# A scan and a routed expert layer on one core: x laid out in zero-padded blocks, one product per two heads, routing pieces placed last in a tile

## The chip, the core and the metric

The kernel runs on one core of a Trainium2 chip. The core has five engines that run side by side and meet through semaphores: TensorE (matrix products, with a queue of its own for weight loads), VectorE, ScalarE, GpSimd and SyncE, which here only issues DMA transfers. [...] Times are microseconds of device time for one execution. In the views, PE is TensorE, PEld its weight loads, DVE is VectorE, ACT is ScalarE, POOL is GpSimd and SP is SyncE; a letter q behind a name is that engine's sequencer. L556 is line 556 of the kernel before.

## What is computed

Two layers follow one another. The first is a chunked state-space scan over 4 batches, 8 heads, 768 positions, with 32 values and 16 states per head. The second sends each of the 3072 tokens, with the 8 x 32 = 256 values that the scan gives for it, to one of 8 experts by a hash of its token id, and applies that expert's two matrices with a ReLU between.

```python
# scan, per batch and head, chunks of 32 positions
cum = np.cumsum(la, axis=-1)                       # la = log(clip(a, 1e-6, 1))
L = np.exp(cum[:, :, :, None] - cum[:, :, None, :]) * causal
M = np.einsum('bhin,bhjn->bhij', Cc, Bc) * L
y_intra = np.einsum('bhij,bhjd->bhid', M, xc)
y_inter = np.einsum('bhin,bhnd->bhid', Cc, state) * np.exp(cum)[:, :, :, None]
y[:, :, sl] = y_intra + y_inter
state = decay_full * state + sum_j(Bc * xc * decay_from_j)

# routing: x is (3072, 256), w1 (8, 256, 1024), w2 (8, 1024, 256), all float32
expert_idx = token_ids * 2654435761 % 8            # the multiplier is 1 modulo 8
h = np.maximum(xe @ w1[e], 0.0)
out[mask] = h @ w2[e]
```

## The kernel before, in words

**The scan** works with chunks of 64 positions (`HL`), 12 to a batch (`NU`). A tile is two chunks, 128 positions; the loop over `gc` (L603) runs over 24 tiles, `b` being the batch and `c` the tile in it, 0 to 5. In each tile TensorE computes the grams of the next tile (L530: B times C, 32 rows by 64 columns of the array, four side by side), VectorE multiplies them with the causal mask into `m` (L534), and then `outputs(gc)` makes the tile's result. It has two kinds of product, both into the tile `y_ps`: L547, the state of the chunk before (`ups`, 64 rows) against C with its decay (`cps`), and L556, x (`xs`, 64 rows) against `m`. Heads 0 to 3 lie on partitions 0 to 63 and heads 4 to 7 on 64 to 127; the index `q` says which. So a product uses a 64 x 64 quarter of the array, and the two `q` and the two chunks `u` of a tile fill the four quarters. ScalarE copies `y_ps` to `y_sb` (L560), and SyncE writes that to `y_tokens` in DRAM (L561). `y_ps` is two banks of PSUM with one buffer.

Beside this, each tile of batch b does a part of the preparation of batch b + 1: `turn_b` at c = 0 (TensorE turns B, ScalarE copies it), `turn_steps` at c = 1 and 4 (TensorE turns B back, copy `bs`, L447 on VectorE or L449 on ScalarE), `turn_c` at c = 2 (ScalarE makes `ct` and `ce`, then GpSimd makes `cp`, L480, in one operation of 128 x 768), `states` at c = 3 and 5 (L496 on TensorE, then a chain of six on VectorE, L501 and L503), `blocks` (L518 on ScalarE). GpSimd multiplies B and C of the batch after with their factors (`rows`, L431, 96 x 1024, at c = 3 and 5). x, B and C are loaded by SyncE, in the order of the program between the writes of y.

**The routing** is a generator, `routing()` (L218 to L359): small VectorE operations that count tokens per expert and give each a slot, cut by `yield` into pieces. `next(todo)` runs one piece; in the loop it stands right behind `outputs` (L611), so a piece's VectorE operations come ahead of the tile's preparation. The piece of gc = 4 ends at L305, that of gc = 8 makes `egr` (L331 to L334), the table that says which expert each place works on, and that of gc = 17 makes the indices (L357). At gc = 17 two tiles of tokens for the first place are gathered from `y_tokens` (GpSimd's indirect DMA), and at gc = 22 and 23 they are turned.

**The experts.** There are nine places v: place 0 is expert 0 with 256 tokens, places 1 to 7 are the other experts by size (420 down to 372 tokens), place 8 is expert 0 again with 172. For each of the 8 slices f, `up` (L682) makes h and `down` (L692), two slices behind, adds to `o_ps`, two banks with one buffer. At the end of a place, ScalarE copies the one half of `o_ps` and VectorE the other (L701, L703). Weights lie in three buffers of 16 KB per partition in the pool `wpool`. Place 0's are loaded by ScalarE's queue during the scan (L643), places 1 and 2's by SyncE behind units u = 0 and 5 (`load_after`, which first copies one element of h into the buffers so that the load waits), and place v + 3's once place v is done (L696); so place 8's go into a buffer again. GpSimd scatters finished rows to the output.

What sets the order is the program text alone: a fixed order is asked for (L86), and every engine follows it.

At the head of the program VectorE clears small constants (L145, L175, L176) and then takes `a_t` when its DMA lands (L362); a chain over ScalarE, VectorE and TensorE makes the decay factors `fac` and `step` (L412) out of it, which `rows` and all that comes later need.

Of the kernel before, what the change touches and what calls it, by code (L numbers as in the profile page):

```python
# [20 lines left out]
def kernel(  # L21
# [43 lines left out]
    route = pool(ctx, "route", 1)  # L65
    wpool = pool(ctx, "wpool", 1)
    early = pool(ctx, "early", 1)
# [15 lines left out]
    ps_g = pool(a_ctx, "ps_g", 2, space=PSUM)  # L83
    ps_y = pool(a_ctx, "ps_y", 1, space=PSUM)
    fixed_order = tc.manual_schedule()
# [8 lines left out]
    def load_bc(b):  # L94
# [4 lines left out]
        bcs[b] = t  # L99

    def load_x(b, i=None):

        if i in (None, 0):
            xs[b] = aload.tile([P, G, NU, D], F32, name="x_t", bufs=3)
        n = G if i is None else 2
        for h in range(0, H, n) if i is None else (2 * i,):
            q, g = divmod(h, G)
            nc.sync.dma_start(out=xs[b][q * HL:(q + 1) * HL, g:g + n].rearrange("j h k d -> j (h k) d"),
                              in_=x[b, h:h + n].rearrange("h s d -> (h s) d").rearrange("(c j) d -> j c d", j=HL))
# [11 lines left out]

    def new_w(v):
        w1s[v] = wpool.tile([P, DP, F], F32, name="w1", bufs=NWB)
        w2s[v] = wpool.tile([P, FP, DM], F32, name="w2", bufs=NWB)

    def load_w(v, eng, parts=range(4)):

        if v not in w1s:
            new_w(v)
        for i in parts:  # L130
            src, dst, n = ((moe_w1, w1s, DP), (moe_w2, w2s, FP))[i // 2]
            ks = slice(i % 2 * n // 2, (i % 2 + 1) * n // 2)
            if v % E == 0:
                src = src[0].rearrange("(k p) f -> p k f", p=P)
            else:
                if v not in expert:
                    expert[v] = nc.values_load(egr[0:1, v:v + 1], engines=[ET.SP], min_val=0, max_val=E - 1)
                src = src[bass.ds(expert[v], 1)].rearrange("o (k p) f -> p (o k) f", p=P)
            eng.dma_start(out=dst[v][:, ks], in_=src[:, ks])


    ident = const.tile([P, P], F32)
    make_identity(nc, ident)
    ones = const.tile([P, P], F32)
    nc.vector.memset(ones, 1.0)  # L145


# [30 lines left out]
    def spin(moving, n=1):  # L178

        t = ps_y.tile([P, 2, 512], F32, name="y_ps")  # L180
        for _ in range(n):
            nc.tensor.matmul(out=t[:, 0, 0:moving.shape[-1]], lhsT=ident[0:moving.shape[0]], rhs=moving,
                             start=True, stop=True)
# [34 lines left out]
    def routing():  # L218
# [51 lines left out]
        for i in range(2):  # L270
# [58 lines left out]
        nc.vector.tensor_scalar(out=eov, in0=eov, scalar1=E - 1, scalar2=None, op0=OP.bitwise_and)  # L329
        yield  # L330
        nc.vector.tensor_tensor(out=more, in0=at_g.rearrange("p v g -> p g v"), in1=iota_v.unsqueeze(1).to_broadcast(vv),  # L331
                                op=OP.mult)
        nc.vector.tensor_reduce(out=ek[:, 0:V], in_=more, axis=AX.X, op=OP.add)
        nc.vector.tensor_copy(out=egr, in_=ek[:, 0:V])  # L334

# [22 lines left out]
        first = idx_in[:, 0:UPTO[1]]  # L358
        nc.vector.tensor_scalar(out=first, in0=first, scalar1=T0 * P - 1, scalar2=None, op0=OP.min)  # L359


# [17 lines left out]
    totx = apre.tile([NR, BH, NS], F32)  # L379
    step = const.tile([P, NB, NU], F32)  # L380

    nc.gpsimd.tensor_copy(out=totx, in_=tot.unsqueeze(2).to_broadcast([NR, BH, NS]))
# [23 lines left out]
    def steps():  # L406
        step_ps = ps_t.tile([P, 512], F32, name="tp")
        for b in range(NB):
            nc.tensor.matmul(out=step_ps[:, b * NU:(b + 1) * NU],
                             lhsT=totx[:, b * H:(b + 1) * H].rearrange("p h n -> p (h n)"), rhs=step_w,  # L410
                             start=True, stop=True)
        nc.scalar.activation(step.rearrange("p b k -> p (b k)"), step_ps[:, 0:NB * NU], AF.Exp)  # L412

    par = const.tile([P, 2], F32)
# [13 lines left out]
    def rows(b, i, eng):  # L428

        t = abat.tile([NR, RS, P], F32, name="rows", bufs=2)  # L430
        eng.tensor_tensor(out=t.rearrange("p r (h n) -> p h r n", h=H), in0=bcs[b][:, i],  # L431
                          in1=fac[:, i, b * H:(b + 1) * H].unsqueeze(3).to_broadcast([NR, H, RS, NS]), op=OP.mult)
        rws[b, i] = t
# [34 lines left out]
    def turn_c(b, first=False):  # L468
        ct = abat.tile([P, NR, RS], F32, name="ct", bufs=1)
        ce = abat.tile([P, 2, NR, RS], F32, name="ce")  # L470
        for rs, v in turned(b, 1):
            nc.scalar.activation(ct[:, :, rs], v, AF.Copy)  # L472
            if not first:
                for e in range(2):
                    nc.scalar.activation(ce[:, e, :, rs], v, AF.Identity, scale=par[:, e:e + 1])
        for ps in (slice(0, 2 * RU), slice(2 * RU, NR)) if first else ():
            for e in range(2):
                nc.scalar.activation(ce[:, e, ps], ct[:, ps], AF.Identity, scale=par[:, e:e + 1])
        cp = abat.tile([P, NU, HL], F32, name="cp")
        nc.gpsimd.tensor_tensor(out=cp, in0=ct.rearrange("p (k c) r -> p k (c r)", c=RU),  # L480
                          in1=step[:, b].unsqueeze(2).to_broadcast([P, NU, HL]), op=OP.mult)
        ces[b], cps[b] = ce.rearrange("p e (k c) r -> p e k (c r)", c=RU), cp

    def states(b, half):
# [6 lines left out]
        for i in range(n):  # L491
            k = half * UH + i
            for r in range(G):
                q, g = divmod(r, 2)
                w = slice(q * HL, (q + 1) * HL)
                nc.tensor.matmul(out=tp[32 * r:32 * r + 32, i * PW:(i + 1) * PW], lhsT=bs[w, k, 32 * g:32 * g + 32],  # L496
                                 rhs=xb[w, 2 * g:2 * g + 2, k], start=True, stop=True)
        for i in range(n):
# [39 lines left out]
    def outputs(gc):  # L538
        b, c = divmod(gc, R)
        m = ms.pop(gc)  # L540
        y_ps = ps_y.tile([P, 2, 512], F32, name="y_ps")
        for q in range(2):
            w = slice(q * HL, (q + 1) * HL)
            for u in range(2):
                k = 2 * c + u
                if k:
                    nc.tensor.matmul(out=y_ps[u * HL:(u + 1) * HL, q, 0:P], lhsT=cps[b][w, k],  # L547
                                     rhs=ups[b][w, k].rearrange("p g x -> p (g x)"), start=True, stop=False,
                                     skip_group_check=True)
        for h in range(G):  # L550
            g, e = divmod(h, 2)
            for q in range(2):
                w = slice(q * HL, (q + 1) * HL)
                for u in range(2):
                    k = 2 * c + u
                    nc.tensor.matmul(out=y_ps[u * HL:(u + 1) * HL, q, h * D:(h + 1) * D], lhsT=m[w, g, u, e],  # L556
                                     rhs=xs[b][w, h, k], start=(k == 0 and h == 0), stop=(h == G - 1),
                                     skip_group_check=True)
        y_sb = awork.tile([P, 2, P], F32, name="y_sb", bufs=8)
        nc.scalar.activation(y_sb, y_ps[:, :, 0:P], AF.Copy)  # L560
        nc.sync.dma_start(out=y_dram[gc * P:(gc + 1) * P, :], in_=y_sb.rearrange("p q d -> p (q d)"))  # L561

# [40 lines left out]
    for gc in range(NCH):  # L603
# [5 lines left out]
        if gc == 0:  # L609
            states(0, 1)  # L610
        next(todo, None)  # L611

        if c == 1:
            blocks(b, UH + 1, NU)
        if nb < NB:
# [11 lines left out]
            else:  # L627
                states(nb, 1)
        if gc < 2:
            load_x(1, 2 + gc)  # L630
# [55 lines left out]
    def down(v, f):  # L686
        n = CAPS[v]
        if f == 0:
            oP[v] = ps_o.tile([P, DP, 512], F32, name="o_ps")
        h = hT.pop((v, f))  # L690
        for j in range(DP):
            nc.tensor.matmul(out=oP[v][:, j, 0:n], lhsT=w2s[v][:, f, j * P:(j + 1) * P], rhs=h,  # L692
                             start=(f == 0), stop=(f == FP - 1))
        if f == FP - 1:
            if v + NWB < V:
                load_w(v + NWB, nc.sync)  # L696
            op = oP.pop(v)
            for j in range(DP):
                o = oT[:, j, BEG[v]:BEG[v + 1]]
                if j % 2 == 0:  # L700
                    nc.scalar.activation(o, op[:, j, 0:n], AF.Copy)  # L701
                else:
                    nc.vector.tensor_copy(out=o, in_=op[:, j, 0:n])  # L703

# [10 lines left out]

    def load_after(v, f):

        new_w(v)
        nc.vector.tensor_copy(out=w1s[v][0:1, 0, 0:1], in_=hT[0, f][0:1, 0:1])
        nc.vector.tensor_copy(out=w2s[v][0:1, 0, 0:1], in_=hT[0, f][0:1, 0:1])  # L720
        load_w(v, nc.sync)
# [6 lines left out]
    for u in range(V * FP + LAG):  # L728
        v, f = divmod(u, FP)
        if v < V:  # L730
            up(v, f)
        if u in (0, 5):
            load_after(1 + u // 5, u)
# [94 lines left out]
```

## Time and profile before

| | |
|---|---|
| Median of 3 executions | 285.62 us (282.88 to 291.94) |
| The profiled execution: time, span | 287.67 us, 285.9 us |
| TensorE busy | 262.2 us (92%), 2677 products |
| Weight loads busy | 180.2 us (63%), 2677 |
| VectorE, ScalarE, GpSimd busy | 96.5, 65.9, 80.5 us |
| Scan, until the first expert product | 0 to 91.1 us |
| Experts, to the last product's end | 91.1 to 279.5 us |
| Last scatters and end | 279.5 to 285.9 us |
| L556, 768 products, busy | 19.5 us |
| L547, 176 products, busy | 12.0 us |
| cp on GpSimd, 4 times | 1.49 us median |
| rows on GpSimd, 6 times | 1.94 us median |

Each float32 product of the program appears as two in the profile, with two weight loads. [...]several are under way at a time, so the distance from the start of one group to the start of the next says more than the mean duration. Groups of like instructions are merged in the timeline: start, duration of the group, engine, line, operation, output and inputs, shape, count. A bracket at the end of a line gives the idle time of the engine before it and what ended it.

### The profile page before, as it was taken

Reading aid. Unit: us, or ns where it says so; the run is one execution under the profiler, and the core shown is the slowest. Engines: PE = TensorE matmul, PEld = TensorE weight load, DVE = VectorE, ACT = ScalarE, POOL = GpSimd, SP = SyncE. Lnnn points to the kernel's source line nnn. Section 1 sums busy time; section 2 is a strip of 40 time slices with the busy share of each in tenths; the row PEclk is TensorE's granted clock in tenths of the full one; section 3 lists DMA queues with packets and bytes.
Section 4 is the critical chain, followed back from the end, with each engine's and each line's share of the span. In section 5 each row is a group of like instructions: output and inputs, shape, how many; then the busy total and the mean of one; then the engine's idle time right before and its main releaser. Section 6 shows DMA issues by size and latency. Waiting matters only on the chain.

```text
span 285.9 us, 6492 instructions
## 1 busy us (share of the span) xinstructions
PE 262.2 (92%) x2677; PEld 180.2 (63%) x2677; DVE 96.5 (34%) x229; ACT 65.9 (23%) x155; POOL 80.5 (28%) x114
## 2 busy tenths in 40 slices
PE   8779859979879999999999999999999999999990
PEld 7667648868757876555555565555566566566780
DVE  2756896695632131121121231121113112112110
ACT  4534613647331101101110111111210211110120
POOL 6650250354300720240160052044035022012042
PEclk9987965999995899999999999999999999999997
DMA  6994993654351799323424415413432441001010
GB/s 126 145 134 97 183 199 76 118 156 141 106 170 58 232 337 348 117 64 148 147 87 170 149 55 178 152 52 117 168 114 83 158 153 55 0 17 37 2 54 34
DMA packets 52178, 35.28 MB, mean 123 GB/s; under 512 B 29817, under 2 KB 48274, under 8 KB 52148
## 3 DMA queue, kind: packets, MB, share of 16 engines
q1 hardware_dynamic: 48404, 26.34, 35.5%
q0 software_dynamic: 2400, 6.43, 6.9%
q10 hardware_dynamic: 1344, 2.10, 2.4%
q8 instruction: 21, 0.34, 0.5%
q14 instruction: 9, 0.07, 0.1%
HBM read 28.57 MB, written 6.42 MB: 122 GB/s over the span
## 4 chain that ended last, share of the span: by engine, by line
issue 47%; DMA 11%; POOL 10%; PE 1%; POOLq 1%; ACT 0%; ACTq 0%
DMA out_dram<-o_sb,idx_out 9%; POOL xg L566 7%; POOL out_dram L661 3%; DMA y_tokens<-y_sb 1%; PE y_ps L556 1%; PE y_ps L547 0%; PE gram L530 0%; POOLq L566 0%; ACT y_sb L560 0%; POOLq L661 0%; POOLq L754 0%; ACTq L560 0%
## 5 line engine op out<-in xcount | busy, mean ns | idle before, releaser
L682 PE MATMUL h_ps<-xT,w 128*128 128x256 f32 (+8 forms) x288 | 99.8, 471 | 1.0 <-DVE xT L579 1.0
L692 PE MATMUL o_ps<-hT,w 128*128 128x256 f32 (+8 forms) x288 | 98.2, 465 | 0.6 <-DVE oT L703 0.6
L692 PEld LDWEIGHTS o_ps<-hT,w 128*128 128x128 f32 x288 | 52.9, 190 | 34.9 <-issue 9.6
L682 PEld LDWEIGHTS h_ps<-xT,w 128*128 128x128 f32 x288 | 52.6, 195 | 27.1 <-issue 7.6
L661 POOL DMA_INDIRECT out_dram<-o_sb,idx_out x25 | 25.2, 1008 | 133.5 <-ACT o_sb L711 78.1
L675 DVE TENSOR_SCALAR hT<-h_ps 128x256 f32<-128x256 f32 (+8 forms) x36 | 19.0, 528 | 80.5 <-PE h_ps L682 80.5
L673 ACT ACTIVATE hT<-h_ps 128x256 f32<-128x256 f32 (+8 forms) x36 | 16.8, 467 | 98.0 <-PE h_ps L682 98.0
L566 POOL DMA_INDIRECT xg<-y_tokens,idx_in x25 | 25.7, 1028 | 25.5 <-PE h_ps L682 14.2
L579 DVE COPY xT<-xt_ps 128x256 f32<-128x256 f32 x23 | 9.8, 425 | 49.1 <-PE xt_ps L577 49.1
L556 PE MATMUL y_ps<-x_t,m 64*64 64x32 f32 x768 | 19.5, 235 | 3.8 <-issue 3.8
L534 DVE TENSOR_TENSOR m<-gram,causal 128x512 f32<-128x512 f32 x24 | 16.5, 688 | 14.5 <-PE gram L530 14.4
L530 PE MATMUL gram<-ce,bt 32*64 32x128 f32 x384 | 19.5, 316 | 1.8 <-issue 1.8
L556 PEld LDWEIGHTS y_ps<-x_t,m 64*64 64x64 f32 x768 | 18.7, 156 | 2.7 <-issue 2.7
L560 ACT ACTIVATE y_sb<-y_ps 128x256 f32<-128x256 f32 x24 | 9.3, 388 | 35.5 <-PE y_ps L556 27.0
L530 PEld LDWEIGHTS gram<-ce,bt 32*64 32x64 f32 x384 | 12.4, 151 | 4.6 <-issue 2.7
L480 POOL TENSOR_TENSOR cp<-ct,step 128x768 f32<-128x768 f32 x4 | 6.3, 1584 | 30.1 <-ACT ct L472 30.1
L431 POOL TENSOR_TENSOR rows<-bc,fac 96x1024 f32<-96x1024 f32 x6 | 12.4, 2072 | 5.1 <-DMA bc<-in_B_dram 3.0
L711 ACT ACTIVATE o_sb<-ot_ps 128x256 f32<-128x256 f32 x13 | 5.0, 384 | 37.0 <-PE ot_ps L708 37.0
L503 DVE SCALAR_TENSOR_TENSOR st<-st,step,tp 128x64 f32<-128x64 f32 x40 | 11.2, 281 | 4.3 <-PE tp L496 3.0
L518 ACT ACTIVATE up<-st,hm 128x160 f32<-128x160 f32 (+1 forms) x32 | 11.3, 426 | 4.4 <-POOL rows L431 3.2
L547 PE MATMUL y_ps<-up,cp 64*64 64x128 f32 x176 | 12.0, 325 | 0.1
L496 PE MATMUL tp<-x_t,bs 64*32 64x64 f32 x352 | 8.0, 242 | 3.8 <-DVE bs L447 3.6
(147 smaller groups left out, 176.6 us busy)
## 6 DMA issues: line engine op xcount, KB each, us to landing
w<-in_moe_w_dram SPq DMA_DIRECT2D x32, 512.0 KB, 4.3
y_tokens<-y_sb SPq DMA_DIRECT2D x24, 128.0 KB, 2.9
x_t<-in_x_dram SPq DMA_DIRECT2D x12, 192.0 KB, 4.4
w<-in_moe_w_dram ACTq DMA_DIRECT2D x4, 512.0 KB, 4.2
bc<-in_B_dram SPq DMA_DIRECT2D x4, 384.0 KB, 5.4
bc<-in_C_dram SPq DMA_DIRECT2D x4, 384.0 KB, 5.1
x_t<-in_x_dram SPq DMA_DIRECT2D x2, 384.0 KB, 9.7
xg<-y_tokens,idx_in POOLq DMA_INDIRECT x25, 2.8
```

Of the source, the lines that this page charges most:

```text
L431: eng.tensor_tensor(out=t.rearrange("p r (h n) -> p h r n", h=H), in0=bcs[b][:, i], in1=fac[:, i, b * H:(b + 1) * H].unsqueeze(3).to_broad ...
L518: nc.scalar.activation(ups[b][:, k0:k1, g, ds], sts[b][:, k0:k1, ds], AF.Identity, scale=hm[:, g, e:e + 1])
L530: nc.tensor.matmul(out=gram[q * HL:(q + 1) * HL, g, u * P:(u + 1) * P], lhsT=bts[b][rr, 2 * c + u], rhs=ces[b][rr, :, 2 * c + u], start=Tr ...
L534: nc.vector.tensor_tensor(out=m.rearrange("p g u e i -> p g (u e i)"), in0=gram[:, :, 0:2 * P], in1=causal.rearrange("p (g x) i -> p g (x ...
L547: nc.tensor.matmul(out=y_ps[u * HL:(u + 1) * HL, q, 0:P], lhsT=cps[b][w, k], rhs=ups[b][w, k].rearrange("p g x -> p (g x)"), start=True, s ...
L556: nc.tensor.matmul(out=y_ps[u * HL:(u + 1) * HL, q, h * D:(h + 1) * D], lhsT=m[w, g, u, e], rhs=xs[b][w, h, k], start=(k == 0 and h == 0), ...
L566: nc.gpsimd.indirect_dma_start(out=dst, out_offset=None, in_=y_dram[0:n, :], in_offset=bass.IndirectOffsetOnAxis(ap=idx, axis=0), bounds_c ...
L661: st = nc.gpsimd.indirect_dma_start(out=out[:], out_offset=bass.IndirectOffsetOnAxis(ap=idx, axis=0), in_=src, in_offset=None, bounds_chec ...
L673: nc.scalar.activation(o, i, AF.Relu)
L675: nc.vector.tensor_scalar_max(out=o, in0=i, scalar1=0.0)
L682: nc.tensor.matmul(out=hp, lhsT=w1s[v][:, i, f * P:(f + 1) * P], rhs=xv[:, i], start=(i == 0), stop=(i == DP - 1))
L692: nc.tensor.matmul(out=oP[v][:, j, 0:n], lhsT=w2s[v][:, f, j * P:(j + 1) * P], rhs=h, start=(f == 0), stop=(f == FP - 1))
```

## The change

- x goes into one tile `xall` of 3 x 4 x 12 x 2 x 32 values per partition: for each of three batch slots, head g and chunk k there are two blocks of 32 columns, and the block `q` is filled on the half `q` of the partitions only. The other block is zero; six memsets on VectorE, ahead of all but one of its instructions, write these zeros once.
- L547 and L556 become products over all 128 rows and 64 columns. `cp` exists twice, once per `q`, with zeros on the other half's partitions (from `step2`, which is `step` with zeros); the product with `q` fills the columns of `q`. L556 does heads h and h + 4 in one product of 64 columns, `m` over all 128 rows against x with zeros. The order of the columns in `y_ps` becomes head, q, value, and ScalarE's copy turns it back. There are 8 products of the second kind in a tile instead of 16, and still 4 of the first.
- `y_ps` becomes one bank with two buffers, and `o_ps` two tiles of one bank.
- GpSimd's `cp` is six operations of 128 x 256, its `rows` four of 96 x 256 (batches 1 to 3).
- `next(todo)` moves to the end of the tile's preparation, and the `egr` piece behind the indices, to gc = 17; the pieces between come one tile earlier.
- Expert 0's weights get a buffer of their own for the whole program and are not loaded a second time. The other three buffers move to a pool that takes the place of the scan's tiles; place 3 is loaded behind unit 10.

```diff
+    xall = apre.tile([P, 3, G, NU, 2, D], F32)
...
-            xs[b] = aload.tile([P, G, NU, D], F32, name="x_t", bufs=3)
+        xs[b] = xall[:, b % 3]
...
-            nc.sync.dma_start(out=xs[b][q * HL:(q + 1) * HL, g:g + n].rearrange("j h k d -> j (h k) d"),
+            nc.sync.dma_start(out=xs[b][q * HL:(q + 1) * HL, g:g + n, :, q].rearrange("j h k d -> j (h k) d"),
...
+    new_w(0, early, 1)
+    w1s[E], w2s[E] = w1s[0], w2s[0]
...
     nc.vector.memset(ones, 1.0)
+    for i in range(3):
+        for q in range(2):
+            nc.vector.memset(xall[q * HL:(q + 1) * HL, i, :, :, 1 - q].rearrange("j h k d -> j (h k) d"), 0.0)
...
+    step2 = const.tile([P, 2, NB, NU], F32)
+    nc.vector.memset(step2, 0.0)
...
         nc.scalar.activation(step.rearrange("p b k -> p (b k)"), step_ps[:, 0:NB * NU], AF.Exp)
+        for q in range(2):
+            w = slice(q * HL, (q + 1) * HL)
+            nc.scalar.activation(step2[w, q].rearrange("p b k -> p (b k)"), step_ps[w, 0:NB * NU], AF.Exp)
...
-        eng.tensor_tensor(out=t.rearrange("p r (h n) -> p h r n", h=H), in0=bcs[b][:, i],
-                          in1=fac[:, i, b * H:(b + 1) * H].unsqueeze(3).to_broadcast([NR, H, RS, NS]), op=OP.mult)
+        n = H if b == 0 else 2
+        for h in range(0, H, n):
+            hs = slice(b * H + h, b * H + h + n)
+            eng.tensor_tensor(out=t.rearrange("p r (h n) -> p h r n", h=H)[:, h:h + n], in0=bcs[b][:, i, h:h + n],
+                              in1=fac[:, i, hs].unsqueeze(3).to_broadcast([NR, n, RS, NS]), op=OP.mult)
...
-        cp = abat.tile([P, NU, HL], F32, name="cp")
-        nc.gpsimd.tensor_tensor(out=cp, in0=ct.rearrange("p (k c) r -> p k (c r)", c=RU),
-                          in1=step[:, b].unsqueeze(2).to_broadcast([P, NU, HL]), op=OP.mult)
+        cp = abat.tile([P, 2, NU, HL], F32, name="cp")
+        for k in range(0, NU, 4):
+            for q in range(2):
+                nc.gpsimd.tensor_tensor(out=cp[:, q, k:k + 4], in0=ct.rearrange("p (k c) r -> p k (c r)", c=RU)[:, k:k + 4],
+                                        in1=step2[:, q, b, k:k + 4].unsqueeze(2).to_broadcast([P, 4, HL]), op=OP.mult)
...
-        y_ps = ps_y.tile([P, 2, 512], F32, name="y_ps")
+        y_ps = ps_y.tile([P, 512], F32, name="y_ps")[:, 0:2 * P].rearrange("p (h q d) -> p h q d", h=G, q=2)
         for q in range(2):
-            w = slice(q * HL, (q + 1) * HL)
             for u in range(2):
                 k = 2 * c + u
                 if k:
-                    nc.tensor.matmul(out=y_ps[u * HL:(u + 1) * HL, q, 0:P], lhsT=cps[b][w, k],
-                                     rhs=ups[b][w, k].rearrange("p g x -> p (g x)"), start=True, stop=False,
+                    nc.tensor.matmul(out=y_ps[u * HL:(u + 1) * HL, :, q], lhsT=cps[b][:, q, k],
+                                     rhs=ups[b][:, k].rearrange("p g (e d) -> p (g e) d", e=2), start=(q == 0), stop=False,
                                      skip_group_check=True)
         for h in range(G):
             g, e = divmod(h, 2)
-            for q in range(2):
-                w = slice(q * HL, (q + 1) * HL)
-                for u in range(2):
-                    k = 2 * c + u
-                    nc.tensor.matmul(out=y_ps[u * HL:(u + 1) * HL, q, h * D:(h + 1) * D], lhsT=m[w, g, u, e],
-                                     rhs=xs[b][w, h, k], start=(k == 0 and h == 0), stop=(h == G - 1),
-                                     skip_group_check=True)
+            for u in range(2):
+                k = 2 * c + u
+                nc.tensor.matmul(out=y_ps[u * HL:(u + 1) * HL, h], lhsT=m[:, g, u, e], rhs=xs[b][:, h, k],
+                                 start=(k == 0 and h == 0), stop=(h == G - 1), skip_group_check=True)
...
         outputs(gc)
         if gc == 0:
             states(0, 1)
-        next(todo, None)
...
                 states(nb, 1)
+        next(todo, None)
...
-            oP[v] = ps_o.tile([P, DP, 512], F32, name="o_ps")
+            oP[v] = [ps_o.tile([P, 512], F32, name=f"o_ps{j}") for j in range(DP)]
...
-            if v + NWB < V:
+            if 0 < v and v + NWB < E:
+                new_w(v + NWB, mwork, NWB)
                 load_w(v + NWB, nc.sync)
...
-        if u in (0, 5):
+        if u in (0, 5, 10):
             load_after(1 + u // 5, u)
```

## The prediction

> **What bounds the kernel now.** I read the page's rows of busy tenths first, then TensorE's own timeline through the scan, then VectorE's timeline where TensorE stands still.
>
> The page's 40 slices are of 7.15 us:
>
> ```profile
> PE   8779859979879999999999999999999999999990
> DVE  2756896695632131121121231121113112112110
> PEclk9987965999995899999999999999999999999997
> ```
>
> TensorE is busy from slice 13 (about 91 us) to the end: the expert stage, 91 to 281 us, is TensorE at full rate. The change's main edits lie ahead of 91 us, where TensorE has holes, VectorE is busy for more than half, and the clock row drops twice: in the slices from 43 us and from 86 us. The page's chain follows GpSimd's scatters and calls 47% of itself "issue", so it says nothing of the scan; I go by TensorE's timeline (start, duration, line, shape, count, idle before and its releaser):
>
> ```profile
> 33.43 0.91 PE L444 MATMUL tp<-ident,bt 64*64 64x64 f32 x24
> 34.27 0.44 PE L530 MATMUL gram<-ce,bt 32*64 32x128 f32 x6
> 36.26 0.65 PE L530 MATMUL gram<-ce,bt 32*64 32x128 f32 x10 [1.55 <-issue]
> 36.84 0.45 PE L547 MATMUL y_ps<-up,cp 64*64 64x128 f32 x8
> 37.11 0.98 PE L556 MATMUL y_ps<-x_t,m 64*64 64x32 f32 x32
> 41.13 1.29 PE L496 MATMUL tp<-x_t,bs 64*32 64x64 f32 x40 [3.04 <-DVE bs L447]
> 42.35 1.13 PE L530 MATMUL gram<-ce,bt 32*64 32x128 f32 x16
> ...
> 51.03 0.45 PE L547 MATMUL y_ps<-up,cp 64*64 64x128 f32 x8
> 51.30 0.62 PE L556 MATMUL y_ps<-x_t,m 64*64 64x32 f32 x32
> 51.85 0.88 PE L459 MATMUL tp<-ident,rows 96*128 96x96 f32 x8
> ...
> 56.29 0.91 PE L444 MATMUL tp<-ident,bt 64*64 64x64 f32 x24
> 57.13 0.67 PE L530 MATMUL gram<-ce,bt 32*64 32x128 f32 x16
> ...
> 84.66 0.74 PE L556 MATMUL y_ps<-x_t,m 64*64 64x32 f32 x26 [1.84 <-issue]
> 85.33 1.13 PE L530 MATMUL gram<-ce,bt 32*64 32x128 f32 x16
> ```
>
> Three things are to be seen. From 51 us the instructions follow each other without holes, some 2.2 us a tile: there the scan is bound by TensorE's own work. Holes come from two sources: "issue" (1.45 us before 21.13, the 1.55 and 1.84 above, and 0.17, 0.37, 0.23 at 58.4, 75.6, 79.0: 5.6 us), and late VectorE results (3.04 us). After a long hole the same 16 grams cost 1.13 us instead of 0.67: half clock, about 23.5 to 26.5, 36 to 51 and 85 to 94 us. Counting rows, 766, 1020, 1020, 256 and 256 instructions (products and weight loads) lie between one "issue" hole and the next: multiples of 256 within the missing records.
>
> VectorE around the 3.04 us hole:
>
> ```profile
> 35.88 1.79 DVE L298 SCALAR_TENSOR_TENSOR jump<-jump,tabv 128x9 f32<-128x9 f32 x1
> ...
> 38.19 1.99 DVE L303 TENSOR_TENSOR val<-val,start 128x216 f32<-128x216 f32 x1
> 40.22 0.38 DVE L305 SCALAR_TENSOR_TENSOR cnt<-val,jump 128x216 f32<-128x216 f32 x1
> 40.52 0.55 DVE L447 COPY bs<-tp 128x384 f32<-128x384 f32 x1
> ```
>
> The bs copy stands behind a routing piece. Two operations of that piece last until GpSimd's rows products (35.70 to 37.64, 37.89 to 39.95) end; a like one on 216 elements costs 0.38.
>
> [...]
>
> **The change part by part**, against the profiled execution: span 285.9, time 287.67 us, which is 2.05 above the median of the three runs.
>
> *Six memsets of xall, 64 x 1536, at the head of VectorE's queue: +5.9.* The rows of the two full-width memsets (165 ns for 128 elements, 272 for 256) give 0.84 ns an element, so 165 + 1408 x 0.84 = 1.35 us each[...]. I take 1.45: 8.7 us. They stand ahead of the turn0 memsets (0.46) and of a_t's clip, which starts at 4.32 when its DMA lands. New start 1.05 + 8.7 + 0.46 = 10.2. Behind it, each waiting for the last, are Ln, the scan, rel, the exponentials, the first rows and everything else; the waits there are 0.5 to 0.7 us, and nothing covers 5.9. [...] The x loads don't wait for the memsets (other columns). step2's memset and two activations (0.1 to 0.2 each) fall into waits of 0.5 us: nothing. GpSimd's constants behind totx move along; its next work is also later.
>
> *Outputs with 128 rows: +7.9.* Before, L547 is 8 instructions in two rounds of four 64x64 tiles, 0.27 us from start to next start (0.135 a round); L556 is 32, 0.55. After, L547 has 8 in four rounds of two column halves: 4 x 0.135 = 0.54. L556 has 16 in eight rounds of two with N=64; L444 has that form (24 instructions, twelve rounds of two, 0.84 us): 0.070 a round, 0.56. So 1.10 for 0.82 us: I take +0.33 over 24 tiles, some of the old 0.55 being the change of tile shape (0.44 before an L444). Half the instructions, but twice the streamed zeros. That two column halves over the same rows run side by side is seen at L496 (64*32: 48 instructions in 0.81 us, a sole one of 64 columns costing at the experts' 0.84 ns 0.054). Low end, loads all hidden: 0.43 + 0.43, +0.1 a tile, +2.4. High end, no load hidden: a load costs 0.027 (L556, two per row half in a 0.055 round), so (0.107 + 0.055) x 4 + (0.053 + 0.055) x 8 = 1.5, +18. A new change of shape before L444 in 8 tiles: 0.11 each, +0.9. Where TensorE then waits for VectorE anyway (c = 5 of batch 0 and the next two), 1.5 comes back.
>
> *Routing last in a tile, GpSimd in pieces: -4.5.* bs now goes ahead of the piece, so 3.04 goes, and with it the half clock from 36 to 51 us (0.46 a gram, 0.25 L547, 0.45 L556, 0.5 to 0.65 the turns: 5.3). Late next: m. VectorE's pieces at c = 3, 4 and 5 are some 1.9, 1.6 and 1.2 us plus waits for GpSimd, and m of the tiles after stands behind them; outputs wait for it. I count waits of about 1 us in two or three tiles[...]. Ends: 0 and -8.3. A rows piece of 256 columns is 1.94 / 4 = 0.49 us, so one VectorE operation waits at most that, but several may; cp doubles to 6 x 0.5 = 3 us, and cp's users come three tiles later: nothing. The table egr is needed only by the weight loads after 91 us: nothing on SP.
>
> *Fewer TensorE instructions: -5.6.* 768 of 5354 go (384 products, 384 loads). [...] I take half of the 5.6 us of holes and half of the 5.7 of half clock behind the first and last (1.2 and 4.5). Ends: 0 and -11.3.
>
> *y_ps in one bank, twice: -1.3.* The waits of L547 for y_sb are 1.3 in all. *o_ps apart: -1.2.* Between experts the products stand 1.33 to 1.35 apart for 1.25, eight times, plus 0.57 at 269.6. *Expert 0 kept: 0.* Four loads of 512 KB on SP go; v = 8 was loaded by 228 us and used at 264. The experts' buffers now overlay the scan's, so their first copy on VectorE also waits for the y writes; those land at 92.4, ahead of hT at 93.7. Behind it stand relu copies with three h_ps buffers. Expert 3's load moves from unit 9 to 10 and is used at 24.
>
> Sum: 5.9 + 7.9 + 0.9 - 1.5 - 4.5 - 5.6 - 1.3 - 1.2 = +0.6. Own time 288.3; against the median 286.2.
>
> **Rivals.** *Weight loads show* (ends slower): [...]outputs cost up to 0.75 more a tile: 286.2 + 10 = 296. For: L556 is at its load rate now. Against: the experts' 128-row loads hide wholly. It decides from 0.54 a tile (+13). *All holes go*: both ranges above at their ends, 286.2 - 3.8 - 5.7 = 276.7. [...] Against: later waits for m are as long as holes that halved the clock before. *The reorder does nothing*: the wait only moves from bs to m and the clock stays down in batch 1: 286.2 + 4.5 = 290.7.
>
> **How the numbers follow.** My sum 0.43 (own range 281 to 291), loads show 0.25, all holes go 0.2, reorder void 0.12. Two per cent, 5.7 us, is about what can be told from no change: under 279.9 faster, over 291.3 slower. Faster 0.2; slower 0.3, with a share of the edges; same 0.5. The range 279 to 296 leaves out the lower half of "all holes go" and the top of "loads show".
>
> **What would show it.** Right: a_t's clip near 10 us after six memsets of about 1.4; L547's successor near 0.54 and L556's near 0.56 in warm tiles; no wait for bs, but waits for m; "issue" holes fewer or shorter. Wrong: memsets well under 1 us, an outputs pair above 1.3 or below 0.9, or the grams at 0.67 from 36 us on.

## The result and the profile after

The changed kernel takes 293.19 us (median of 4 executions, 292.28 to 294.75), the kernel before 285.57 (4 executions, 282.88 to 291.94). The ratio is 1.0305, 95% interval 1.021 to 1.0399: slower by 3%. Medians count all executions; the ratios leave out those more than 1.5% above the quickest of their kernel, and of the profiles below, those of before, of the GpSimd piece ahead of cp, of the reorder alone and of the second quarters version are of such slow executions. The profiled execution of the changed kernel took 294.75 us, span 292.8 (before: 287.67 and 285.9). Line numbers are those of the kernel that a view is of.

The page's busy tenths of TensorE and its clock, in 40 slices, here of 7.3 us (PEclk is the granted clock in tenths):

```profile
PE   5199987999498959999999999999999999999991
PEclk9557999999799989999999999999999999999996
```

The clock dips of before in the slices from 43 and 86 us are gone. New are an almost empty slice at 7 us with half clock behind it, a hole at 73 us and one at 102. The head first, on VectorE's timeline (start, duration, line, operation, shape, count, idle before):

```profile
1.32 1.34 DVE L150 MEMSET xall<- 64x1536 f32 x1 [0.26 <-issue]
3.02 1.34 DVE L150 MEMSET xall<- 64x1536 f32 x1 [0.36 <-issue]
...
9.81 1.34 DVE L150 MEMSET xall<- 64x1536 f32 x1 [0.36 <-issue]
11.24 0.27 DVE L180 MEMSET turn<- 96x256 f32 x1
11.59 0.38 DVE L367 SCALAR_TENSOR_TENSOR a_t<-a_t,ones 96x256 f32<-96x256 f32 x1
```

A memset lasts 1.34 us, but the next starts 1.70 after it. The clip of a_t comes at 11.59 instead of 4.32. TensorE's timeline at the other places:

```profile
13.29 0.50 PE L376 MATMUL tp<-cum,rel_w 96*96 96x32 f32 x2 [7.71 <-DVE cum L372]
...
17.86 1.66 PE L472 MATMUL tp<-ident,rows 96*128 96x96 f32 x8
...
44.54 0.68 PE L568 MATMUL y_ps<-xall,m 128*64 128x64 f32 x15 [1.70 <-DVE m L549]
...
53.45 0.66 PE L561 MATMUL y_ps<-up,cp 128*64 128x128 f32 x8
53.94 0.63 PE L568 MATMUL y_ps<-xall,m 128*64 128x64 f32 x16
54.50 0.88 PE L472 MATMUL tp<-ident,rows 96*128 96x96 f32 x8
...
76.94 1.16 PE L353 MATMUL tp<-of,at 128*128 128x50 bf16 x24 [3.89 <-POOL of L349]
78.03 1.13 PE L545 MATMUL gram<-ce,bt 32*64 32x128 f32 x16
...
107.46 0.69 PE L588 MATMUL xt_ps<-ident,xg 128*128 128x128 f32 x2 [3.12 <-DMA xg<-y_tokens,idx_in]
```

The outputs of a warm tile now take 0.49 and 0.56 us from start to start (before: 0.27 and 0.55); a product of L568 lasts 224 ns on the mean, and 16 of them start within the 0.56 us. Between 26 and 75 us the clock never falls, and no hole called "issue" is left there. In their place are two new waits. The first is for GpSimd, whose timeline shows why:

```profile
72.28 3.46 POOL L495 TENSOR_TENSOR cp<-ct,step 128x256 f32<-128x256 f32 x6 [3.22 <-ACT ct L485]
75.70 1.18 POOL L349 TENSOR_TENSOR of<-of,one_ub 128x600 bf16<-128x600 bf16 x1
```

The product for the index table stands behind the last batch's six cp operations, and TensorE, in whose queue the index product (L353) has moved up by one tile, waits for it. Before, it stood behind cp too, but cp was one operation, and TensorE came for the table a tile later and waited 0.59 us:

```profile
69.75 1.47 POOL L480 TENSOR_TENSOR cp<-ct,step 128x768 f32<-128x768 f32 x1 [2.66 <-ACT ct L472]
71.18 1.19 POOL L349 TENSOR_TENSOR of<-of,one_ub 128x600 bf16<-128x600 bf16 x1
```

The second wait is at the start of the experts. Before, on all engines' timelines:

```profile
93.44 1.00 POOL L566 DMA_INDIRECT xg<-y_tokens,idx_in  x1 [14.15 <-PE h_ps L682]
...
93.92 18.74 SPq L139 DMA_DIRECT2D w<-in_moe_w_dram  x12
```

and after:

```profile
99.15 12.89 SPq L138 DMA_DIRECT2D w<-in_moe_w_dram  x7
...
99.88 1.00 POOL L577 DMA_INDIRECT xg<-y_tokens,idx_in  x1 [13.90 <-DVE hT L686]
```

The first gather of the second place's tokens now starts 0.7 us after the start of the 2 MB load of that place's weights, not 0.5 us ahead of it, and its tokens are used 7.6 us later. Before, the first twelve h_ps products ran at half clock (4.87 us); now they take 2.86, and the place needs its tokens sooner.

Where the difference of the two profiled executions arises, by the start of the same instruction in both:

| instruction | before | after | shift |
|---|---|---|---|
| clip of a_t | 4.32 | 11.59 | +7.3 |
| grams of tile 1 | 18.22 | 27.02 | +8.8 |
| grams of tile 16 | 68.02 | 70.53 | +2.5 |
| grams of tile 18 | 73.96 | 81.41 | +7.5 |
| first expert product | 91.09 | 97.16 | +6.1 |
| first product of the second place | 106.85 | 115.84 | +9.0 |
| last group of o_ps products | 276.22 | 283.49 | +7.3 |

So the scan's middle gives back 6.3 us of the 8.8 lost in the head; then 4.9 are lost around the index product, 1.4 come back, 2.9 are lost at the gathers, and 1.7 come back in the experts.

Part of this belongs to the one profile of before. A run below changes that kernel only behind the start of the experts, and its profiled execution took 283.15 us: there the grams of tiles 1, 16 and 18 start at 18.40, 67.15 and 73.09, the clock stays up from 47 us to the experts, and the first expert product comes at 87.08, 4.0 us earlier than in the table. Against it the first shifts are +8.6, +3.4, +8.3 and +10.1. So the 1.4 us that come back ahead of the experts are the half clock that the profile of before had there, and not a gain of the change.

### The profile page after: what moved, and what is told of

Its sections match the earlier page's. It is cut to its first block, busy times and chain, and to the rows that moved or that the text cites. A ratio compares the mean times of both kernels' runs of the same rounds, so it can differ in the third digit from the quotient of the medians.

```text
span 292.8 us, 5776 instructions
## 1 busy us (share of the span) xinstructions
PE 262.9 (90%) x2293; PEld 181.9 (62%) x2293; DVE 101.9 (35%) x238; ACT 65.9 (23%) x157; POOL 92.2 (31%) x152
## 4 chain that ended last, share of the span: by engine, by line
issue 49%; POOL 15%; PE 14%; DMA 11%; DVE 8%; ACT 1%; POOLq 1%; SPq 0%; DVEq 0%; ACTq 0%
DMA out_dram<-o_sb,idx_out 9%; POOL xg L577 7%; PE gram L545 3%; POOL out_dram L672 3%; DVE xall L150 3%; PE y_ps L561 2%; POOL cp L495 2%; POOL rows L444 2%; PE y_ps L568 2%; DVE st L518 2%; PE tp L472 2%; DMA xall<-in_x_dram 2%; PE tp L511 1%; PE tp L457 1%; PE y_ps L187 1%
## 5 line engine op out<-in xcount | busy, mean ns | idle before, releaser
L703 PEld LDWEIGHTS o_ps<-hT,w 128*128 128x128 f32 x288 | 54.0, 192 | 32.9 <-issue 10.2
L495 POOL TENSOR_TENSOR cp<-ct,step 128x256 f32<-128x256 f32 x24 | 14.6, 643 | 25.0 <-ACT ct L485 14.8
L568 PE MATMUL y_ps<-xall,m 128*64 128x64 f32 x384 | 17.0, 224 | 4.4 <-DVE m L549 4.1
L568 PEld LDWEIGHTS y_ps<-xall,m 128*64 128x64 f32 x384 | 15.1, 138 | 5.6 <-DVE m L549 5.1
L545 PE MATMUL gram<-ce,bt 32*64 32x128 f32 x384 | 17.4, 293 | 0.3 <-issue 0.3
L444 POOL TENSOR_TENSOR rows<-bc,fac 96x256 f32<-96x256 f32 x24 | 16.3, 711 | 0.6 <-DMA bc<-in_B_dram 0.6
L561 PE MATMUL y_ps<-up,cp 128*64 128x128 f32 x176 | 16.2, 291 | 0.2 <-DVE up L527 0.2
L561 PEld LDWEIGHTS y_ps<-up,cp 128*64 128x64 f32 x176 | 10.3, 140 | 4.5 <-issue 3.2
L588 PEld LDWEIGHTS xt_ps<-ident,xg 128*128 128x128 f32 x46 | 6.5, 144 | 10.3 <-issue 4.6
L545 PEld LDWEIGHTS gram<-ce,bt 32*64 32x64 f32 x384 | 11.0, 138 | 2.7 <-issue 0.5
```

What stands on the lines that cost most here:

```text
L495: nc.gpsimd.tensor_tensor(out=cp[:, q, k:k + 4], in0=ct.rearrange("p (k c) r -> p k (c r)", c=RU)[:, k:k + 4], in1=step2[:, q, b, k:k + 4] ...
L545: nc.tensor.matmul(out=gram[q * HL:(q + 1) * HL, g, u * P:(u + 1) * P], lhsT=bts[b][rr, 2 * c + u], rhs=ces[b][rr, :, 2 * c + u], start=Tr ...
L561: nc.tensor.matmul(out=y_ps[u * HL:(u + 1) * HL, :, q], lhsT=cps[b][:, q, k], rhs=ups[b][:, k].rearrange("p g (e d) -> p (g e) d", e=2), s ...
L568: nc.tensor.matmul(out=y_ps[u * HL:(u + 1) * HL, h], lhsT=m[:, g, u, e], rhs=xs[b][:, h, k], start=(k == 0 and h == 0), stop=(h == G - 1), ...
L703: nc.tensor.matmul(out=oP[v][j][:, 0:n], lhsT=w2s[v][:, f, j * P:(j + 1) * P], rhs=h, start=(f == 0), stop=(f == FP - 1))
```

## The experiments

Two theories went in. H: the time was lost by the order of queues (six memsets ahead of VectorE's chain, one product behind cp on GpSimd), while dearer products and fewer holes about cancel. P: the 128-row products cost it. The first three runs and the first of the quarters shared one chip, the others three more; on these four the kernel before had medians of 286.60, 285.81, 288.03 and 286.51 us, so I lean on positions in the traces.

The page holes of the expectations are the holes called issue: between one and the next the prediction counts close to multiples of 256 TensorE rows, and the queue q8, kind instruction, has 21 packets (0.34 MB) in the profile of before and 19 (0.31 MB) in that of after. What makes the holes was not shown.

### The memsets moved to GpSimd

```diff
-            nc.vector.memset(xall[q * HL:(q + 1) * HL, i, :, :, 1 - q]..., 0.0)   # 6, at the head
+    zeros(0)             # 2 on GpSimd, behind its constants
...
     rows(1, 1, nc.gpsimd)
+    zeros(1)             # 4 on GpSimd
+    zeros(2)
```

> The changed kernel with its six memsets on GpSimd instead of VectorE: slot 0's two behind GpSimd's constants (about 11 us), the other four behind the rows of batch 1. Theory H (the head of VectorE's queue and one GpSimd queue cost the time): a_t's clip is back near 4.3 us, the first loop gram comes 7 to 9 us earlier than at 27.0, and the time is 284 to 286.5. Theory P (the 128-row products cost it, the memsets are hidden behind other waits): over 290.

288.02 us (287.19 to 288.54), some 5 less than the changed kernel, and less gain than H asked. The grams of tile 1 came at 21.42 us, 5.6 earlier than in the changed kernel but still 3.2 later than before. Waits of 3.90 (GpSimd) and 2.05 us (gathers) stayed. So the memsets cost, and the new place isn't free either; more on that with the last placing.

### The GpSimd piece ahead of cp

```diff
+        if gc == 14:
+            next(todo)
         if c == 1:
             blocks(b, UH + 1, NU)
...
-        next(todo, None)
+        if gc != 14:
+            next(todo, None)
```

> The changed kernel, with the one routing piece of gc = 14 (GpSimd's second product for the index table) put back ahead of the tile's preparation, so that it stands before cp in GpSimd's queue. H: TensorE's wait of 3.89 us for it at 76.9 goes, and the half clock behind it, so 287.5 to 289.5. P: the wait only moves on, 292 to 294.

288.66 us, as H has it. The index product starts after a hole of 0.15 us instead of 3.89 and runs at full clock; the grams behind stay at 0.67. P's picture, a wait that only moves on, is out. The run with the reorder alone, below, splits the wait: there cp is one operation of 1.47 us as before, and TensorE, coming a tile earlier, waits 2.11 us. The rest of the 3.89 is about what the doubled cp lasts longer (3.46 us for 1.47).

### Both

> Both of the edits above. H: the gains add, 279 to 283; the wait for the gathers at the start of the experts (3.1 us in the changed kernel) stays or grows. P: 288 or more.

281.76 us (280.80 to 283.58): the gains add, as H has it, with the 128-row products still in. The wait for the gathers stayed, 3.33 us.

### The memsets alone, in the kernel before

```diff
     nc.vector.memset(ones, 1.0)
+    pad = apre.tile([P, G, NU, 2, D], F32)
+    for i in range(3):
+        for q in range(2):
+            nc.vector.memset(pad[q * HL:(q + 1) * HL, :, :, (i + q) % 2]..., 0.0)
```

> The kernel before, with six memsets of 64 x 1536 on VectorE at the changed kernel's place, on a tile that nothing reads. H: the head shifts by 7.3 us and nothing covers it: 292 to 295. If the later start lets x's loads finish and a page hole goes: 288 to 291.

292.42 us, ratio to before 1.0194 (1.0098 to 1.0291): about 5.5 us by the ratio (the interval is 2.8 to 8.3). TensorE's timeline of this run:

```profile
13.31 0.50 PE L375 MATMUL tp<-cum,rel_w 96*96 96x32 f32 x2 [7.26 <-DVE cum L371]
...
26.23 0.67 PE L534 MATMUL gram<-ce,bt 32*64 32x128 f32 x16
...
42.54 0.65 PE L534 MATMUL gram<-ce,bt 32*64 32x128 f32 x10 [2.48 <-issue]
...
69.69 0.67 PE L534 MATMUL gram<-ce,bt 32*64 32x128 f32 x16
...
86.39 0.59 PE L560 MATMUL y_ps<-x_t,m 64*64 64x32 f32 x26 [1.84 <-issue]
86.91 0.67 PE L534 MATMUL gram<-ce,bt 32*64 32x128 f32 x16
```

The head is as late as in the changed kernel, and the hole that lay near 20 us before is not there; the later "issue" holes are. Both expectations hold in part: most of the shift arrives at the end, and some comes back by the first hole; whether x's loads had a part in it was not shown. The same memsets therefore cost about the same without any of the other edits.

The run shows one thing more. Its grams of tiles 1 and 16 stand 43.46 us apart, in the changed kernel 43.51, in the two profiles of before's scan 49.80 and 48.75. So what the changed kernel gets back in the middle of the scan comes with the later head alone, with all the quarters, the old order and whole GpSimd operations in place.

### The weights of the second place later: in the changed kernel, before, and with both mends

```diff
-        if u in (0, 5, 10):
+        if u in (4, 5, 10):
             load_after(1 + u // 5, u)
```

> The changed kernel with the same edit, and the memsets and the GpSimd order as the change has them. If the wait of 3.1 us for xg and the half clock behind it are a third part of what the change lost: 4 to 5 us less than 293.2, so 288 to 289.5. If the wait is covered by something else: 292 to 294.

291.06 us (290.37 to 291.32); ratio to before 1.015 (1.0097 to 1.0204), where the changed kernel had 1.0305: 1.5%, 4.4 us. The median itself lies between the two expected ranges, only 2.1 us under the changed kernel's, on another chip. The wait for xg is gone, and the second place starts 14.79 us after the first (97.12 and 111.91) where it took 18.68. So this is the third part of the loss.

> The kernel before, with the second place's weights started at unit 4 instead of unit 0. In its profile the first gather went ahead of that load (93.44 and 93.92 us) and nothing waited for xg, but its first expert products ran at half clock. If the gathers race with the load in this kernel too and lose in its quicker executions: 1 to 3 us less, 282.5 to 285. If it is only the changed kernel that loses the race: no change.

286.61 us; ratio 0.9871 (0.9758 to 0.9985), some 3.7 us, of uncertain size. The kernel before runs the same race: wherever its first expert products ran at full clock, they met the wait (3.79 us in the run with the memsets alone, 4.11 in the run with the reorder alone, below). In the profile of before the gather went first by 0.5 us, and the place took 2.0 us more at half clock; which of the two hid the wait was not tried apart. The first quarters version, below, had both again (gather 0.2 us ahead of the load, half clock) and no wait.

> As the one with both edits, with the first load behind the scan (the second place's weights) started at unit 4 instead of unit 0. If the gathers of the second place's tokens are late because they share the DMA engines with that load: the wait of 3.3 us for xg goes, and the half clock behind it, so 276.5 to 279. If the gathers are late by themselves (their own 1.3 us a piece, the last y write): no change, or more, as the weights come late at unit 8.

276.98 us (276.21 to 278.49); ratio 0.9668 (0.9603 to 0.9732). In the trace:

```profile
83.35 2.86 PE L700 MATMUL h_ps<-xT,w 128*128 128x256 f32 x12 [0.52 <-DVE xT L592]
...
97.10 1.68 PE L700 MATMUL h_ps<-xT,w 128*128 128x420 f32 x4 [0.52 <-DVE xT L592]
```

13.75 us for the first place, with no wait for xg. This version beats both kernels: the change with its three costs mended. Against the kernel before with the same late load, the ratios are 0.9668 and 0.9871, so some 2% belong to the change itself, by two ratios from different chips, whose intervals don't meet.

### What the central edit is worth: quarters again

```diff
-        y_ps = ps_y.tile([P, 512], F32, name="y_ps")[:, 0:2 * P]...
+        y_ps = ps_y.tile([P, 2, 512], F32, name="y_ps")            # one buffer
...
-                nc.tensor.matmul(out=y_ps[u * HL:(u + 1) * HL, h], lhsT=m[:, g, u, e], rhs=xs[b][:, h, k], ...)
+            for q in range(2):       # w: the half q of the partitions
+                nc.tensor.matmul(out=y_ps[u * HL:(u + 1) * HL, q, h * D:(h + 1) * D], lhsT=m[w, g, u, e],
+                                 rhs=xs[b][w, h, k, q], ...)
```

Once on the version with two mends:

> As the one with both edits, but the output products are again 64 x 64 quarters (16 and 4 in a tile, no zeros used) and y_ps is two banks with one buffer. If the 128-row products cost what the starts show (1.05 for 0.82 us a tile) and nothing else changes: 5.5 us less than with both edits. If the smaller number of TensorE instructions is what keeps the page holes away: holes called issue of over 1 us return, with half clock behind them, and it is 2 to 6 us more. P: at least 9 us less.

286.69 us (284.23 to 290.15) beside 281.76 on the same chip. And once on the version with three mends and another place for the first memsets:

> The same, with the output products as 64 x 64 quarters again. With the head, the GpSimd order and the gathers out of the way, this is the price of the change's central edit by itself. By the starts alone (1.05 for 0.82 us a tile): 5 us less than with 128 rows. If twice the output instructions bring the page holes and the half clock back: 2 to 7 us more.

281.62 us, ratio to before 0.9808 (0.9697 to 0.9919), beside 277.44 and 0.973 (0.9659 to 0.9801) of the same version with 128 rows. The intervals overlap, so the size is not settled. By the executions that the ratios count it is 279.63 for 277.44, and 286.22 for 281.76 in the first pair. The direction is the same both times, and both times against the starts alone, which promise 5 us less. The clock of the second pair, quarters first:

```profile
PEclk9977979999655999999999999999999999999997
```

```profile
PEclk9869999999999999999999999999999999999998
```

With quarters, "issue" holes stand in TensorE's timeline again (1.00 before 21.01 us, 1.44 before 35.99, 0.86 before 69.52), and the clock is at half from about 71 us to the experts. With 128 rows, two of 0.3 us and one of 0.2 are left, and the clock stays up. The first pair shows the same at the first expert products, quarters first:

```profile
88.76 5.26 PE L704 MATMUL h_ps<-xT,w 128*128 128x256 f32 x12 [0.52 <-DVE xT L596]
```

```profile
85.47 2.86 PE L700 MATMUL h_ps<-xT,w 128*128 128x256 f32 x12 [0.52 <-DVE xT L592]
```

The whole difference lies in the stretch with this late half clock. From the grams of tile 1 to those of tile 16 it is 42.24 and 43.42 us with quarters, 43.96 and 43.45 with 128 rows; from there to the first expert product 25.65 and 25.73 against 20.88 and 21.56. So a tile costs 0.23 us more and the scan less. That the smaller number of products keeps the clock up is likely, but argued and not shown: the holes just ahead of the half clock are of 0.2 to 0.9 us, and the run with the memsets alone, also with quarters, took 21.03 us there at full clock, behind holes of 0.78 and 1.84. The quarters also put back the one buffer of y_ps; that is hardly the cause, since weight loads waited for y_sb only 0.5 and 0.3 us with quarters, and 0.3 without.

### The order of the routing pieces alone, in the kernel before

```diff
         outputs(gc)
         if gc == 0:
             states(0, 1)
-        next(todo, None)
...
                 states(nb, 1)
+        next(todo, None)          # and the egr piece to the end
```

> The kernel before, with the routing pieces at the end of a tile's preparation and the egr piece last, and nothing else of the change. If the order of the pieces is what keeps the clock up between 36 and 51 us: no wait for bs, waits for m of 1 to 2 us in its place, 281 to 284. If the page holes alone rule the clock: the holes called issue stay near 20, 35 and 82 us with half clock behind them, 284 to 287. The index matrix product waits longer for GpSimd (cp now ahead of it), some 1.5 us.

287.79 us; ratio 1.0084 (1.0034 to 1.0133). No gain, if anything a loss. On TensorE:

```profile
38.40 0.65 PE L530 MATMUL gram<-ce,bt 32*64 32x128 f32 x10 [2.53 <-issue]
41.27 1.13 PE L530 MATMUL gram<-ce,bt 32*64 32x128 f32 x16
...
58.11 0.67 PE L556 MATMUL y_ps<-x_t,m 64*64 64x32 f32 x32 [1.94 <-DVE m L534]
...
73.38 1.07 PE L348 MATMUL tp<-of,at 128*128 128x50 bf16 x24 [2.11 <-POOL of L344]
```

The wait for bs is gone, as both theories had it; the holes and the half clock behind them are not, a wait for m and one for GpSimd have come. The wait for GpSimd doesn't hide a gain: from the grams of tile 1 to those of tile 16, ahead of it, the run took 51.11 us, and the profiles of before's scan 49.80 and 48.75. The reorder by itself kept nothing warm.

### GpSimd whole instead of in pieces

```diff
-        n = H if b == 0 else 2
+        n = H
...
-        for k in range(0, NU, 4):       # cp: six operations of 128 x 256
+        for q in range(2):              # two of 128 x 768
```

> As the one with both edits, but GpSimd's cp in two operations of 128 x 768 and rows whole again. If the pieces matter to VectorE[...]: waits for m of 2 to 4 us near 36 to 45 us, half clock, and 2 to 5 us more than with both edits. If they don't: within 1 us.

282.04 us beside 281.76 with pieces: no difference that can be told, though on two chips. TensorE waited 1.94 and 0.37 us for m, where with the pieces it waited 1.39, 1.43 and 0.66. The pieces don't shorten these waits.

### The first memsets in VectorE's own gap

In the version that beats both, VectorE's timeline at 11 us shows the price of the memsets on GpSimd (11.10 to 13.89):

```profile
11.04 1.51 DVE L229 TENSOR_SCALAR eid_i<-tok 24x128 int32<-24x128 int32 x1
12.58 1.39 DVE L231 CAST eid_r<-eid_i 24x128 f32<-24x128 int32 x1
```

Two operations of 0.22 us took 2.9. So one of slot 0's memsets went to VectorE (1.34 us, while it waits for a_t until 4.35) and one to GpSimd ahead of totx:

```diff
+    zeros(0, 0, nc.vector)     # behind ones
...
+    zeros(0, 1, nc.gpsimd)     # behind upto, ahead of totx
```

> The version with all three mends (memsets away from the head, the GpSimd order, the later weight load), with slot 0's two memsets placed otherwise: one on VectorE in its wait for a_t (1.3 to 4.3 us), one on GpSimd ahead of totx. In the version before, two VectorE casts of 24 x 128 took 1.51 and 1.39 us beside GpSimd's memsets, for 0.22. If those memsets hold VectorE up: the casts are back at 0.22, the first loop gram comes 2 to 3 us earlier than at 20.8, and the time is 274 to 275.5. If the head is bound elsewhere: 276.5 to 278.

277.44 us (276.51 to 277.99), ratio 0.973 (0.9659 to 0.9801): no gain, a miss. The casts are back at 0.22 and the grams of tile 1 come 1.3 us earlier (19.46 for 20.78), but the first expert product comes 1.1 later (84.47): the waits for m are 1.75, 1.12 and 1.33 us, where they were 0.92, 1.18 and 0.37. That is 1.7 us more of waiting for VectorE, most of the 2.4 us that went between the two places; what made m late stays open.

## Why the prediction was right and wrong

The range held the time, and slower was given 0.3. But the likeliest case, no change at 286.2, did not happen, and slower came by another road than the rival named for it: weight loads do not show (1.05 us for a tile's outputs, where that rival needed 1.36 or more; in the experts, from 116 to 285 us, loads busy for 103.61 us lie beside products busy for all 169.00). The range reached to 296 for that rival's sake, so that it held the time was luck. The sum said +0.6 against the profiled execution, which moved by +7.1. By its own steps:

- **Six memsets, +5.9: right in place, too small.** The row measures 1.34, as the rows of the kernel's own memsets gave it (1.35); the 1.45 taken was the author's estimate, and no row shows it. The term missed the 0.36 us between two of them: 1.70 x 6 for 1.45 x 6, a clip 7.3 us later. Nothing covered it up to tile 1, and TensorE's half clock in the wake of its 7.71 us wait (0.52 granted from 13 to 26 us) added 1.5 until there. Behind tile 1 a part came back, which the term left out: with the memsets alone, 5.5 us are left at the end.
- **Outputs, +7.9: the mechanism right, a little large.** L561 takes 0.49 for 0.54 forecast, L568 0.56 as forecast: +0.23 a tile over the 0.82 of before, 5.5 us.
- **Routing last, -4.5: wrong by itself.** The waits for m came as counted (1.70, 1.12 and 1.27 us). But the run with the reorder alone gained nothing. The prediction laid the half clock from 36 to 51 us to the wait for bs; the run has half clock behind a hole of 2.53 us without any wait for bs, though only to about 44 us. Whether the hole of 1.55 us would have been enough, and what the wait for bs added, stays open.
- **Fewer instructions, -5.6: not shown.** That half of the holes and of the half clock behind them would go was the author's estimate. Holes called issue fell from 5.6 us to 0.6, and grams of tile 1 to tile 16 took 6.3 us less. But the memsets alone bring as much there, with holes of 4.1 us left in that stretch; only about the 3.5 us that the dearer outputs cost in 15 tiles must have been made good by the other edits. The pairs of quarters and 128 rows say that the edit gains 2 to 5 us in all, behind tile 16.
- **"cp doubles to 6 x 0.5 = 3 us, and cp's users come three tiles later: nothing." This step failed.** It asked who uses cp and not what stands behind it in GpSimd's queue. There stood, before and after, the index table's product, and the reorder brought TensorE to it a tile earlier. The wait went from 0.59 us to 2.11 by the reorder alone and to 3.89 with the longer cp; with half clock behind it (0.66 granted from 75 to 80 us), that cost 4.9 in all. With the piece ahead of cp it is 4.5 less by the medians.
- **Weights and gathers, 0: failed as cover.** The text saw that the experts' first copy comes 1.3 us behind the last y write, and did not see that the gathers, which wait for that write too, then race with the weight load. In the profile of before, the gather went first and the first expert products ran at half clock; one of these, or both, was the cover. In the changed kernel both were gone, and 3.12 us of wait came. The later load gets back 1.5% by the ratios.
- **o_ps apart, -1.2: right.** From the second place's first product to the last o_ps group it is 169.37 us before and 167.65 after, -1.7. **y_ps, -1.3: too large.** The weight loads' waits for y_sb fell from 1.3 us to 0.7, and with one buffer again (the quarters) they are 0.5 and 0.3.

## What to carry to other kernels

When an operation grows on an engine that is "not the bottleneck", read that engine's queue past it: who stands behind it, and who waits for that one. A memset at the head of a queue is paid from its start to the next start, gap included (here 1.70 us for a row of 1.34), if the chain that starts the kernel is behind it; what comes back later has to be looked for, here some 2 of 7.3 us. And take a second profile of the kernel before, and one with each part alone: here 1.4 us ahead of the experts were no gain of the change, and the memsets alone brought back as much in the middle of the scan as the whole change. When an edit makes a stage warm or quick, look at what the slow stage had given time to: here a gather and a weight load race, and every profile in which the expert stage began at full clock with the early load shows the wait.

## What the runs showed of the hardware

- Here zeros were worth multiplying. Column halves with half their rows zero cost 0.23 us a tile more than four quarters (1.05 for 0.82), and yet both versions with them, with 384 products and 384 weight loads fewer, were 2.2 and 4.5 us quicker. Holes called issue were 5.6 us in the profile of before, 0.6 in the changed kernel.
- Holes of 1.44 to 2.94 us mostly had half clock behind them (1.13 for 0.67 us a group of grams), but two of 1.47 and 1.84 us in the run with the memsets alone did not, and single waits of 1.1 to 1.8 us for m between 36 and 50 us mostly left it up too. What decides between them stays open.
- Beside two GpSimd memsets (11.10 to 13.89 us) VectorE's int32 mask operation and cast of 24 x 128 took 1.51 and 1.39 us, the cast ending at 13.97; they took 0.22 each in the run where the memsets stood elsewhere.
- Six like memsets on VectorE start 1.70 us apart with rows of 1.34.
